# A written-out order of all steps in place of a list planner (one core, fp32 attention and gated convolution)

## Chip, core and metric

One NeuronCore of a Trainium2 chip runs the whole program. The metric is device microseconds of one execution; the median of three runs is compared. Engines: PE (TensorE, matrix products), DVE (VectorE), ACT (ScalarE), POOL (GpSimd), SP (SyncE, which only issues transfers here).

## The reference

```python
# x [4, 12800, 128], inducing [32, 128]
def mab(q, kv):
    s = scale * (q @ kv.transpose(0, 2, 1))
    s = s - s.max(-1, keepdims=True)
    a = np.exp(s)
    a /= a.sum(-1, keepdims=True) + 1e-09
    return a @ kv
h = mab(I, x)              # 32 inducing rows attend to all 12800 tokens of a batch
y = mab(x, h)              # every token attends to the 32 rows of h
gate = sigmoid(causal depthwise convolution of y, 5 taps, conv_w)
out = (gate * (y @ w_val)) @ w_out
```

So each batch is read in full (first attention) before its second attention can begin, and everything behind that works on chunks of tokens.

## The kernel before

The 12800 tokens of a batch are four strips of 3200, which lie side by side on the partitions (32 each) or are four 32-wide tiles of the PE array. A strip is cut into chunks (`SIZES`: 8 in batch 0, 7 in the others, at most 480 tokens), 29 in all. The work on a chunk consists of steps, each a Python closure that issues a few instructions on one engine:

- `load_xt`, `load_xk`: the chunk of x with channels on partitions, and with tokens on partitions. In batch 0 the second form of six chunks is made from the first (`make_xk`: PE transposes in `tp`, copies out of PSUM in `ev`).
- `s1`: scores against the inducing rows on PE; DVE copies them out and takes maxima. `gmax`: the maximum of a group of chunks. `e1`: exponential (ACT) and transpose (DVE). `h`: product with x on PE, summed per group in `H` (DVE, `acc`).
- `prep`: joins a batch's groups (ACT scales each `H`, POOL adds them, PE sums over strips) to `hT`. `prep2`, `prep3`: folds `hT` with the convolution taps and w_val into gate and value weights `W`, in two fp16 halves (`e` 0 and 1). `prep_out`: scaled w_out in two halves (`wo`) and the output scale.
- `s2`: second attention of a chunk. PE scores, then eleven steps over DVE, POOL and ACT (`tin, mx, sub, ex, sm, sa, rz, nm, tout, hi, lo`), which end in `P1` and `P2`, the high and low fp16 halves of the weights P.
- `rblock` (r0 to r29): gate products of chunk k (15 per strip, `gate_mm`) with the value products of chunk k - 1 set in (`val_mm`); then tanh of the gate banks (ACT, `th`), gate times value (DVE, `gv`), and the split into halves (`halves`: ACT `hi`, POOL `lo`).
- `outp`: output product of one strip of a chunk (three fp16 products, or one fp32 product in the last chunk), evacuation on DVE or ACT (`ev`), and store.

PSUM has four single banks, `a0` to `a3`, which nearly all of these share, and two double ones, `g0` and `g1`, for the gates (and, early, for the transposes). PE works in three tile shapes: full array, 32-column strips (`s1`, `s2`, `h`, some of `outp`) and 32-row tiles (`rblock`).

`ORDER` lists the PE work by hand, one item for each call above. `('z', k, n)` in it is `idle`: n products of a zero tile into bank g1, whose result nobody reads. `warm_up` issues eight of them before the first data. Each call appends its steps to `Plan.ops` (1547 of them); step numbers follow from that. `Plan.order` keeps the PE order of the list and lays the steps of the other engines and the banks with a table of costs: of the steps that are ready, an engine takes the one with the earliest due time, shifted by `URGE`. A load may be issued from `AHEAD` = 12 blocks ahead. Engines are fixed by the call: `OUTV` lists the evacuations that DVE does, stores go to SP's queue, loads to SP's at first and to ACT's from the first `rblock` on. `manual_schedule` then issues the steps in that order, and each engine runs its own in it.

Of the kernel before, what the change touches and what calls it, by code (L numbers as in the profile page):

```python
# [18 lines left out]
P = 128  # L19
# [18 lines left out]
PASSES = 2  # L38
LAT = dict(PE=0.3, DVE=0.06, ACT=0.045, POOL=0.09, SP=0.05, NOP=0.0)
OVER = dict(DVE=0.075, ACT=0.105, POOL=0.035)  # L40
OWN = 0.035
LAND, LAND_OUT, DEPTH = 4.0, 1.8, 2.4
BESIDE = (3.6, 1.2)
ISSUE = dict(SP=0.45, ACT=0.34)
WINDOW, LEAST = 3.4, 1.95
PAGE, ASK, NEED, LINE, FETCH = 256, 0.68, 1.8, 4.0, 2.5
SWITCH = dict(full=0.09, rows=0.115, strips=0.117)
# [7 lines left out]
class Plan:  # L55


    def __init__(self):
        self.ops = []
        self.tiles = {}  # L60
        self.users = {}
        self.item = -1
        self.urges = {}

    def urge(self, fn):
        code = fn.__code__
        if code not in self.urges:
            self.urges[code] = URGE.get(".".join(fn.__qualname__.split(".")[-3::2]), 0.0)
        return self.urges[code]

    def op(self, eng, dur, fn, deps=(), early=0.0, new=(), use=(), lag=None, kind=None, behind=(), dma=None, words=0):
        i = len(self.ops)
        self.ops.append(dict(eng=eng, dur=dur, fn=fn, deps=[d for d in deps if d is not None], early=early,
                             lag=LAT[eng] if lag is None else lag, kind=kind, behind=list(behind),
                             urge=self.urge(fn), item=self.item, dma=dma, words=words))
# [8 lines left out]
    def order(self, pe):  # L84
        ops = self.ops
        n = len(ops)
        deps = [list(o["deps"]) for o in ops]
        turn = self.turn = set()
        for tag, made in self.tiles.items():
            if tag == "a":  # L90
                continue
            bufs = BUFS[tag]
            for k, (i, key) in enumerate(made):
                if k and made[k - 1][0] != i:
                    deps[i].append(made[k - 1][0])
                    turn.add((made[k - 1][0], i))
                if k >= bufs:
                    deps[i] += [u for u in [made[k - bufs][0]] + self.users[made[k - bufs][1]] if u != i]
        for i, o in enumerate(ops):
            for j in o["behind"]:  # L100
                deps[i].append(j)
                turn.add((j, i))
        runs = []
        for i in pe:
            if not runs or ops[i]["kind"] != runs[-1][0]:
                runs.append((ops[i]["kind"], []))
            runs[-1][1].append(i)
        for k, (kind, run) in enumerate(runs):
            if kind == "either":
                near = [q[0] for q in runs[max(k - 1, 0):k + 2]]  # L110
                for i in run:
                    ops[i]["kind"] = "strips" if "strips" in near else "full"
                    ops[i]["words"] = 24 if "strips" in near else 6
        for a, b in zip(pe, pe[1:]):
            deps[b].append(a)
            ops[a]["turn"] = SWITCH[ops[a]["kind"]] * (ops[a]["kind"] != ops[b]["kind"])
        succ = [[] for _ in range(n)]
        left = [0] * n
        for i, ds in enumerate(deps):
            left[i] = len(ds)  # L120
            for d in ds:
                succ[d].append(i)
        topo, ready = [], [i for i in range(n) if not left[i]]
        cnt = list(left)
        while ready:
            i = ready.pop()
            topo.append(i)
            for s in succ[i]:
                cnt[s] -= 1
                if not cnt[s]:  # L130
                    ready.append(s)
        if len(topo) < n:
            i, seen = next(i for i in range(n) if cnt[i]), []
            while i not in seen:
                seen.append(i)
                i = next(d for d in deps[i] if d not in topo)
            raise AssertionError("a cycle in the plan: " + " <- ".join(
                f"{ops[j]['eng']} {ops[j]['fn'].__qualname__.split('.')[-3]} {[k for l in self.tiles.values() for a, k in l if a == j]}"
                for j in seen[seen.index(i):]))
        nominal, t = {}, 0.0  # L140
        for i in pe:
            nominal[i] = t
            t += ops[i]["dur"] + ops[i].get("turn", 0.0)
        best = None
        for _ in range(PASSES):
            seq, at, end, bank = self.lay(deps, succ, topo, nominal)
            if best is None or max(end) < best[0]:
                best = max(end), seq, at, end, bank
            nominal = {b: end[a] for a, b in zip(pe, pe[1:])} | {pe[0]: 0.0}
        _, seq, self.at, self.end, self.bank = best  # L150
        self.alldeps = deps
        return seq

    def lay(self, deps, succ, topo, nominal):

        ops = self.ops
        n = len(ops)
        late = [max(nominal.values()) + 30.0] * n
        for i in reversed(topo):
            late[i] = nominal.get(i, late[i])  # L160
            for s in succ[i]:
                late[i] = min(late[i], late[s] - ops[i]["dur"] - ops[i]["lag"])
        wants = [[] for _ in range(n)]
        held = {}
        holds = [[] for _ in range(n)]
        for i, key in self.tiles.get("a", []):
            wants[i].append(key)
            held[key] = 1 + len(self.users[key])
            for u in [i] + self.users[key]:
                holds[u].append(key)  # L170
        open_ = [(0.0, b) for b in range(BUFS["a"])]
        bank, gone = {}, {}
        free, bus = dict.fromkeys(("PE", "DVE", "ACT", "POOL"), 0.75), 1.45
        line, slow, ran = 0.0, 8.0, []
        told, asked, held_up = 0, [], 0
        end = [0.0] * n
        at = [0.0] * n
        avail = {}
        left = [len(ds) for ds in deps]
        pools = {}  # L180
        for i in range(n):
            if not left[i]:
                pools.setdefault(ops[i]["eng"], []).append((ops[i]["early"], i))
        seq = []
        while len(seq) < n:
            best = None
            for e, lst in pools.items():
                if not lst:
                    continue
                if e == "ACT":  # L190
                    lst[:] = [(max(r, bus - DEPTH) if ops[i]["dma"] and ops[i]["dma"][1] == "load" else r, i) for r, i in lst]
                start = max(free.get(e, 0.0), min(r for r, _ in lst))
                if e == "PE":
                    w = len(wants[lst[0][1]])
                    if w > len(open_):
                        continue
                    if w:
                        start = max(start, open_[w - 1][0])
                if best is None or start < best[0]:
                    best = (start, e)  # L200
            start, e = best
            lst = pools[e]
            _, i, r = min((late[i] - ops[i]["urge"], i, r) for r, i in lst if r <= start + 1e-9)
            lst.remove((r, i))
            at[i] = start
            end[i] = start + ops[i]["dur"] + ops[i].get("turn", 0.0)
            if e == "PE":
                if start > slow and sum(b - max(a, start - WINDOW) for a, b in ran if b > start - WINDOW) < LEAST:
                    slow = start + WINDOW
                work = end[i] - start  # L210
                if 8.0 < start < slow:
                    end[i] = start + (2 * work if 2 * work < slow - start else work + (slow - start) / 2)
                begun, w, work = told, ops[i]["words"], end[i] - start
                told += w
                while told > PAGE * (len(asked) + ASK):
# [46 lines left out]
def tile_kernel(ctx: ExitStack, tc: tile.TileContext, xt, xk, indT_in, w64, out):  # L262
# [121 lines left out]
    def sp(dur, fn, new, use=(), free=False):  # L384

        i = op("ACT" if blocks else "SP", dur, fn, [ago()], 0.0, new, use, behind=[] if free else queue[-1:], dma=(dur, "load"))
        if not blocks and not free:
            queue.append(i)
# [833 lines left out]
```

## Time and profile before

| | us |
|---|---|
| median of 3 runs | 277.09 |
| lowest, highest | 276.94, 277.39 |
| profiled execution, span from the first to the last instruction | 275.9 |
| PE, DVE, POOL, ACT busy in it | 265.0, 230.7, 207.6, 197.1 |
| HBM read, written | 48.56 MB, 26.21 MB |

The profile is of one execution. Its span is 1.2 us below the median of the runs. Busy times count the instructions of an engine, not the time in which it issues transfers; the end of a matmul is modelled.

### The profile page before, as it was taken

To read this page: it belongs to the slowest core of one execution; us is meant where nothing else is said; L and a number is where in the kernel's file an instruction comes from. 1 tells how busy PE (TensorE), PEld (TensorE's weight loads), DVE (VectorE), ACT (ScalarE), POOL (GpSimd) and SP (SyncE) were. 2 spreads that over 40 slices of the span, in tenths; PEclk is the share of its full clock that TensorE was granted. 3 is DMA by queue.
4 is the path that set the end of the run, shared out by engine and by line. 5 is a ranking of instruction groups with operands and counts; after the bars stand their busy time and mean duration, and the time that the engine had idled before them with its cause. 6 is when DMAs were issued, how large, how long until landed. Compare 5 with 4: busy or idle time off the path is not lost.

```text
span 275.9 us, 11249 instructions
## 1 busy us (share of the span) xinstructions
PE 265.0 (96%) x4730; PEld 148.4 (54%) x4730; DVE 230.7 (84%) x542; ACT 197.1 (71%) x298; POOL 207.6 (75%) x236
## 2 busy tenths in 40 slices
PE   7999998999999999999999999999999999999993
PEld 2568445557646655475445564665554456544541
DVE  1569799879999989898899998979999998896761
ACT  2366369669849786787677877957778887777763
POOL 2000477986699999966986999877999999999550
PEclk9999999999999999999999999999999999999998
DMA  7999999998999799969999879425443234344447
GB/s 250 424 415 383 416 423 380 385 318 293 323 372 403 227 349 393 397 213 369 343 352 323 297 224 377 150 76 209 150 154 122 85 138 155 133 163 152 149 180 281
DMA packets 35378, 75.49 MB, mean 274 GB/s; under 512 B 2816, under 2 KB 26752, under 8 KB 35328
## 3 DMA queue, kind: packets, MB, share of 16 engines
q1 hardware_dynamic: 19120, 42.03, 39.9%
q10 hardware_dynamic: 16208, 32.75, 34.5%
q8 instruction: 37, 0.61, 0.9%
q14 instruction: 13, 0.11, 0.1%
HBM read 48.56 MB, written 26.21 MB: 271 GB/s over the span
## 4 chain that ended last, share of the span: by engine, by line
PE 87%; DVE 4%; ACT 4%; DMA 2%; issue 1%; POOL 1%; SPq 0%; ACTq 0%; DVEq 0%
PE g L845 29%; PE a L958 23%; PE a L751 8%; PE a L553 7%; PE a L487 7%; PE a L854 6%; DMA xt<-in_xt_dram 2%; PE g L462 2%; ACT xk L467 1%; PE g L1010 1%; PE a L677 1%; ACT ss L533 1%; PE a L948 1%; DVE os L971 1%; DVE tg L914 1%
## 5 line engine op out<-in xcount | busy, mean ns | idle before, releaser
L932 POOL TENSOR_TENSOR gl<-tg,gh 128x960 f16<-128x960 f32 (+4 forms) x56 | 104.7, 1882 | 13.1 <-PE a L958 7.5
L845 PE MATMUL g<-P,W 32*128 32x480 f16 (+4 forms) x1740 | 103.1, 345 | 0.8 <-issue 0.7
L845 PEld LDWEIGHTS <-W 32*128 32x128 f16 x1740 | 53.8, 92 | 38.9 <-issue 10.0
L914 DVE SCALAR_TENSOR_TENSOR tg<-tg,a 128x480 f32<-128x480 f32 (+4 forms) x116 | 64.6, 598 | 6.5 <-PE a L854 5.3
L927 ACT CAST gh<-tg 128x960 f16<-128x960 f32 (+4 forms) x56 | 51.9, 928 | 25.5 <-DVE tg L914 23.8
L958 PE MATMUL a<-gh,wo 128*32 128x448 f16 (+6 forms) x632 | 63.1, 348 | 1.0 <-DVE tg L914 1.0
L904 ACT ACTIVATE tg<-g,gsc 128x960 f32<-128x960 f32 (+4 forms) x58 | 55.4, 991 | 3.4 <-PE g L845 3.1
L958 PEld LDWEIGHTS <-wo 128*32 128x32 f16 (+1 forms) x948 | 35.5, 97 | 37.4 <-issue 16.4
L971 DVE TENSOR_SCALAR os<-a,osc 128x480 f32<-128x480 f32 (+4 forms) x64 | 41.1, 667 | 4.9 <-PE a L958 4.7
L958 PE MATMUL a<-gl,wo 128*32 128x448 f16 (+6 forms) x316 | 43.1, 348 | 0.0
L854 PE MATMUL a<-P,W 32*128 32x480 f16 (+4 forms) x348 | 42.1, 344 | 0.6 <-issue 0.5
L831 POOL TENSOR_TENSOR P<-pt,P 128x480 f16<-128x480 f32 (+4 forms) x29 | 29.9, 1036 | 2.3 <-ACT P L824 1.4
L813 POOL TENSOR_TENSOR e<-e,z 128x480 f32<-128x480 f32 (+4 forms) x29 | 27.2, 938 | 5.8 <-DVE z L806 3.6
L973 ACT ACTIVATE os<-a,osc 128x480 f32<-128x480 f32 (+4 forms) x44 | 26.8, 627 | 6.4 <-PE a L958 5.9
L768 POOL TENSOR_TENSOR e<-e,m 128x480 f32<-128x480 f32 (+4 forms) x29 | 27.2, 940 | 5.0 <-DVE m L762 3.3
L553 PE MATMUL a<-xk,et 128*32 128x129 f32 x800 | 29.2, 274 | 0.7 <-DVE tg L914 0.7
L553 PEld LDWEIGHTS a<-xk,et 128*32 128x32 f32 x800 | 25.0, 109 | 6.8 <-issue 1.9
L751 PE MATMUL a<-xt,hT 128*32 128x480 f32 (+4 forms) x232 | 28.0, 541 | 0.0
L487 PE MATMUL a<-xt,indT 128*32 128x480 f32 (+4 forms) x232 | 26.8, 538 | 1.1 <-DMA xt<-in_xt_dram 0.7
L495 DVE TENSOR_SCALAR_CACHE_REDUCE ss<-a 128x480 f32<-128x480 f32 (+4 forms) x29 | 17.2, 600 | 9.2 <-PE a L487 9.1
L774 ACT ACTIVATE e<-e 128x480 f32<-128x480 f32 (+4 forms) x29 | 16.6, 572 | 8.4 <-POOL e L768 8.2
L824 ACT CAST P<-pt 128x480 f16<-128x480 f32 (+4 forms) x29 | 16.2, 561 | 7.2 <-DVE pt L819 5.5
(107 smaller groups left out, 282.5 us busy)
## 6 DMA issues: line engine op xcount, KB each, us to landing
out_dram<-os SPq DMA_DIRECT2D x52, 240.0 KB, 3.1
xt<-in_xt_dram ACTq DMA_DIRECT2D x11, 960.0 KB, 7.4
out_dram<-os SPq DMA_DIRECT2D x44, 224.0 KB, 4.0
xk<-in_xk_dram ACTq DMA_DIRECT2D x9, 967.5 KB, 9.2
xk<-in_xk_dram ACTq DMA_DIRECT2D x7, 903.0 KB, 8.8
xt<-in_xt_dram SPq DMA_DIRECT2D x6, 960.0 KB, 9.9
xt<-in_xt_dram ACTq DMA_DIRECT2D x5, 896.0 KB, 7.5
xk<-in_xk_dram SPq DMA_DIRECT2D x4, 903.0 KB, 13.3
```

The source lines that it names most:

```text
L487: T.matmul(s[32 * r:32 * r + 32, :n], c_["indT"], x[:, o:o + n // 32, r, :], start=True, stop=True)
L553: T.matmul(t[32 * s:32 * s + 32, :P + 1], st["et", b, c][:, 32 * i:32 * i + 32], st["xk", b, q][:, m + i, :], start=j < R, stop=j >= len(b ...
L751: T.matmul(s[32 * r:32 * r + 32, :n], st["hT", b], x[:, m:m + nb, r, :], start=True, stop=True)
L831: G.tensor_tensor(st[p2][:, o:o + n], st[qk][:, :n], st[p1][:, o:o + n], ALU.subtract)
L845: T.matmul(st[f"g{r // 2}", b, c][:, r % 2, :n], st["W", b][q, w, k, :], st[("P1", "P2")[e]][q, o:o + n], start=u == 0, stop=u == len(taps ...
L854: T.matmul(st["a", "v", b, c, r][:, :n], st["W", b][q, w, TAPS, :], st[("P1", "P2")[e]][q, o:o + n], start=u == 0, stop=u == 2)
L904: S.activation(t[:, :, :n], st[f"g{p}", b, c][:, :, :n], AF.Tanh, scale=st["gsc", b])
L914: V.scalar_tensor_tensor(t, t, 1.0, st["a", "v", b, c, r][:, :n], ALU.add, ALU.mult)
L927: S.copy(sb(pw, g1, [P, 2, CW], F16)[:, :, :n], st[tg][:, :, :n])
L932: G.tensor_tensor(sb(pw, g2, [P, 2, CW], F16)[:, :, :n], st[tg][:, :, :n], st[g1][:, :, :n], ALU.subtract)
L958: T.matmul(t[o:o + wide], w[:, e, o:o + wide], st[g][:, q, :n], start=(e, g) == (0, g1), stop=g == g2)
L971: V.tensor_scalar(o, a, st["osc", b], None, ALU.mult)
```

## The change

The planner, its costs and `URGE` are removed. In their place stand three literals: `SEQ`, the numbers of all 1547 steps in the order in which they are issued; `BANKS`, the `a` bank of each step that opens one; `ELSE`, the engine of 120 steps whose engine differs from that of the call. The PE order is now that of `SEQ` too, and differs from `ORDER` (renamed `WORK`, which now only numbers the steps).

`ELSE` does the following:

- all nine `idle` steps of `ORDER` become nothing (16 products of zeros); `warm_up` stays
- output evacuations: 23 from DVE to ACT, 17 from ACT to DVE
- stores: 34 from SP's queue to ACT's, 2 from ACT's to SP's; of the 34, 17 store what DVE has evacuated
- `sa` of 12 chunks from POOL to DVE
- copies of `make_xk`: three from ACT to DVE, one from DVE to ACT; `acc`: three from DVE to ACT; `prep3.f7`: two from ACT to DVE; `prep2.g1`: one from POOL to DVE

In `prep` of batch 0 the last of the four groups is no longer scaled and added by ACT and POOL. PE sums the first three (`f3`) and adds the fourth with a scaled `pick` into the same bank (`f6`). The halves of the last chunk but one go to buffers of tag `ss` instead of `gh` and `gl`. Loads have no limit of blocks any more. In the new `SEQ` the weights' transfer is issued fifth on SP's queue (ninth before), and the second chunk of batch 0 is loaded ahead of the third, the fourth ahead of the fifth.

```diff
-        for i, o in enumerate(ops):
-            for j in o["behind"]:
...
-        for _ in range(PASSES):
-            seq, at, end, bank = self.lay(deps, succ, topo, nominal)
...
+        banks = iter(BANKS)
+        self.bank = {key: int(next(banks)) for i in SEQ for key in ops[i]["new"] if key[0] == "a"}
+        return SEQ
...
+    def issue():
+        return S if plan.now == "ACT" else nc.sync
...
+        last = len(gs) - 1 if b in JOIN else len(gs)
...
-        for g in gs[1:]:
+        for g in gs[1:last]:
...
+        def add(H, w, first, end):
+            t = pt(key) if first else st[key]
+            T.matmul(t[:, :M], H[:, :P], w, start=first, stop=end, skip_group_check=True)
+            T.matmul(t[:, M:2 * M], H[:, P:].broadcast_to([P, P]), w, start=first and end, stop=end, skip_group_check=True)
+
         def f3():
...
+            add(st[Hs[last - 1]], c_["pick"], True, last == len(gs))
...
+        if b in JOIN:
+            pf = ("pf", b)
+
+            def f5():
+                G.tensor_scalar(sb(pw, pf, [P, M]), c_["pick"], st[f_][:, last:last + 1], None, ALU.mult)
+
+            j = op("POOL", 0.26, f5, [i0, i_const], [pf], [f_])
+
+            def f6():
+                add(st[Hs[last]], st[pf], False, True)
...
+    def split(b, c, p):
+
+        late = seqs.index((b, c)) >= len(seqs) - 1 - SPARE
+        return ("tg", b, c, p), ("ss" if late else "gh", "hi", b, c, p), ("ss" if late else "gl", "lo", b, c, p)
...
+            if plan.now == "PE":
+                t = pt(key, (P, 2, 512))[:, 0]
+                for _ in range(n):
+                    T.matmul(t, c_["zero"][:, :P], c_["zero"], start=True, stop=True)
...
+SPARE = 1
+JOIN = (0,)
...
+SEQ = [
+    5, 17, 1, 20, 0, 2, 13, 4, 38, 75, 29, 62, 9, 3, 69, 72, 32, 88, 111, 10, 125, 6, 11, 174, 190, 7, 12, 33, 201,
...
+ELSE = {
+    8: "NOP", 11: "DVE", 16: "NOP", 24: "ACT", 34: "DVE", 36: "DVE", 50: "ACT", 124: "NOP", 140: "NOP", 141: "NOP",
```

## Rows read from the trace of the kernel before

**Rows 1.** Page of the profile: span, busy time, chain by engine.

```profile
span 275.9 us, 11249 instructions
...
PE 265.0 (96%) x4730; PEld 148.4 (54%) x4730; DVE 230.7 (84%) x542; ACT 197.1 (71%) x298; POOL 207.6 (75%) x236
...
PE 87%; DVE 4%; ACT 4%; DMA 2%; issue 1%; POOL 1%; SPq 0%; ACTq 0%; DVEq 0%
```

**Rows 2.** Busy time by stretches (us; instructions; granted clock; DMA share; GB/s).

```profile
35.00:40.00 5.00, 4.89 (x128) 2.21 (x122) 4.65 (x16) 3.00 (x6) 3.63 (x8) 1.00 1.01 422
40.00:45.00 5.00, 4.46 (x112) 2.58 (x103) 4.74 (x14) 4.07 (x9) 4.08 (x7) 1.00 1.02 390
45.00:50.00 5.00, 3.59 (x90) 2.65 (x84) 4.82 (x15) 3.86 (x9) 3.56 (x6) 1.00 1.05 383
50.00:60.00 10.00, 10.00 (x216) 5.69 (x212) 8.19 (x20) 6.84 (x12) 8.35 (x11) 1.00 1.02 349
...
80.00:120.00 40.00, 39.66 (x767) 22.89 (x758) 37.07 (x85) 33.22 (x51) 38.02 (x41) 1.00 0.93 338
...
270.00:276.00 6.00, 1.40 (x6) 0.48 (x4) 0.36 (x1) 1.75 (x3) 0.00 (x0) 0.84 0.72 266
```

**Rows 3.** Groups of instructions by form: products of zeros inside the run.

```profile
L1010 PE MATMUL g<-zero 128*128 128x512 f16 x16 | 5.0, 382 | 0.2
```

**Rows 4.** Timeline (start, length in us), end of batch 0's sum.

```profile
28.66 1.53 POOL L596 TENSOR_TENSOR H<-H 128x129 f32<-128x129 f32 x3 [5.74 <-ACT H L587]
...
28.80 0.28 DVE L563 COPY H<-a 128x129 f32<-128x129 f32 x1
...
29.11 0.41 ACT L591 ACTIVATE H<-H,f 128x129 f32<-128x129 f32 x1 [0.23 <-DVE H L563]
...
30.25 0.41 PE L602 MATMUL a<-pick,H 128*128 128x32 f32 x2
...
30.50 0.39 PE L603 MATMUL a<-pick,H 128*128 128x32 f32 x2
...
31.53 0.19 DVE L611 TENSOR_TENSOR hT<-a,rz 128x32 f32<-128x32 f32 x1
```

**Rows 5.** Timeline, second weight copy and start of r0.

```profile
35.96 1.47 PE L1010 MATMUL g<-zero 128*128 128x512 f16 x4
...
37.93 0.80 ACT L687 COPY W<-a 128x768 f16<-128x768 f16 x1 [0.37 <-PE a L677]
38.01 0.49 POOL L831 TENSOR_TENSOR P<-pt,P 128x160 f16<-128x160 f32 x1
38.02 0.39 ACTq L420 DMA_DIRECT2D xt<-in_xt_dram  x1
...
38.56 0.60 PE L1010 MATMUL g<-zero 128*128 128x512 f16 x2
...
39.10 1.14 PE L845 MATMUL g<-P,W 32*128 32x128 f16 x60
```

**Rows 6.** Timeline, third P chunk, last tanh before r2, start of r2.

```profile
42.11 0.64 DVE L819 STREAM_TRANSPOSE pt<-e 128x480 f32<-128x480 f32 x1
...
47.92 0.79 ACT L904 ACTIVATE tg<-g,gsc 128x640 f32<-128x640 f32 x1
...
49.76 0.39 PE L845 MATMUL g<-P,W 32*128 32x480 f16 x4 [0.68 <-issue]
```

**Rows 7.** Groups by form on DVE and ACT: count, busy us, mean ns.

```profile
L757 DVE STREAM_TRANSPOSE e<-a 128x480 f32<-128x480 f32 x17 | 11.4, 673 | 0.6 <-PE a L516 0.2
...
L762 DVE TENSOR_REDUCE m<-e 128x15 f32<-128x480 f32 x17 | 10.9, 643 | 0.2
...
L824 ACT CAST P<-pt 128x480 f16<-128x480 f32 x17 | 10.0, 589 | 5.5 <-DVE pt L819 3.8 <-PE a L854 1.6
...
L495 DVE TENSOR_SCALAR_CACHE_REDUCE ss<-a 128x448 f32<-128x448 f32 x11 | 6.6, 609 | 1.9 <-PE a L487 1.9
```

**Rows 8.** Timeline of the tail: the wait before the last output products.

```profile
262.80 0.56 PE L958 MATMUL a<-gh,wo 128*128 128x480 f16 x2 [0.97 <-DVE tg L914]
```

More of the change, by code (lines that the diff above doesn't have):

```diff
@@ L37 @@
 SCALE = 1.0 / math.sqrt(P)
[L38 to L47, printed above, removed]
 COST = dict(
@@ L61, in __init__, with op @@
         self.users = {}
[L62 to L71, printed above, removed]
+        self.now = None
+    def op(self, eng, dur, fn, deps=(), new=(), use=(), lag=None, kind=None, dma=None, words=0, alt=None):
         i = len(self.ops)
-        self.ops.append(dict(eng=eng, dur=dur, fn=fn, deps=[d for d in deps if d is not None], early=early,
-                             lag=LAT[eng] if lag is None else lag, kind=kind, behind=list(behind),
-                             urge=self.urge(fn), item=self.item, dma=dma, words=words))
+        self.ops.append(dict(eng=ELSE.get(i, eng), first=eng, dur=dur, fn=fn, deps=[d for d in deps if d is not None], new=list(new),
+                             use=list(use), lag=lag, kind=kind, dma=dma, words=words, alt=alt or {}))
         for key in new:
@@ L82, in op, with order @@
         return i
-    def order(self, pe):
+    def order(self):
         ops = self.ops
[L86 to L98, printed above, removed]
-        for i, o in enumerate(ops):
-            for j in o["behind"]:
-                deps[i].append(j)
-                turn.add((j, i))
-        runs = []
[L104 to L107, printed above, removed]
+        assert sorted(SEQ) == list(range(len(ops)))
+        runs = []
+        for i in SEQ:
+            if ops[i]["eng"] == "PE":
+                if not runs or ops[i]["kind"] != runs[-1][0]:
+                    runs.append((ops[i]["kind"], []))
+                runs[-1][1].append(i)
         for k, (kind, run) in enumerate(runs):
@@ L123, in order @@
[L123 to L139, printed above, removed]
@@ L369, in tile_kernel, with two, copy @@
     ix = {}
+    def two():
+        return V if plan.now == "DVE" else G
+    def copy(dst, src):
+        if plan.now == "ACT":
+            S.copy(dst, src)
+        else:
+            V.tensor_copy(dst, src)
     def sb(pool, key, shape, dt=F32, pad=None):
@@ L380, in tile_kernel, with load @@
     blocks = []
-    queue = []
[L384 to L388, printed above, removed]
-        return i
-    def ago():
-        return blocks[-AHEAD] if len(blocks) >= AHEAD else None
+    def load(dur, fn, new, use=()):
+        return op("ACT" if blocks else "SP", dur, fn, [], new, use, dma=(dur, "load"))
+    def issue():
+        return S if plan.now == "ACT" else nc.sync
     def wid(b, c):
@@ L412, in load_xt @@
         own = key[2] == c
-        early = S if blocks else nc.sync
         def f():
@@ L426, in load_xk, with made, xk_tile, get @@
+    def made(b, c):
+        return max(SIZES[b][c] // 32 - LOADED.get((b, c), NB), 0)
+    def xk_tile(b, c):
+        q, m = shares(b, c)
+        key = ("xk", b, q)
+        new = key not in plan.users
+        def get():
+            if key not in st:
+                sb(pxk, key, [P, CW // 32, P + 1])
+            return st[key]
+        return key, m, get, [key] * new, [key] * (not new)
     def load_xk(b, c):
         n = SIZES[b][c] // 32
+        lo = made(b, c)
+        s = 1 if lo else PARTS[(b, c) >= (1, 4)][1]
@@ L440, in make_xk @@
+        ix["xk", b, c, 1] = load((1.04 if (b, c) >= (1, 4) else 1.0) * (n - lo) * 66048 / BW, f, new, use)
     def make_xk(b, c, eng):
-        n = SIZES[b][c] // 32
+        n = made(b, c)
         xkey, o = xt_of(b, c)
-        q, m = shares(b, c)
-        key = ("xk", b, q)
+        key, m, get, new, use = xk_tile(b, c)
         last = []
         def ones():
-            if q == c:
-                sb(pxk, key, [P, CW // 32, P + 1])
-            G.memset(st[key][:, m:m + n, P:], 1.0)
-        i0 = op("POOL", 0.13, ones, [], 0.0, [key] * (q == c), [key] * (q != c))
+            G.memset(get()[:, m:m + n, P:], 1.0)
@@ L454, in make_xk @@
+        i0 = op("POOL", 0.13, ones, [], new, use)
         for g in range(0, n, 8):
@@ L753, in s2 @@
         i = PE(COST["s"] * n + 0.015, f, [ix["xt", b, c, u], ix["hT", b]], [key], [xkey, ("hT", b)], "strips")
+        soon = dict(DVE=cost("dve", n) + 0.05) if b == 0 and c < 3 else None
         def tin():
```

449 lines of the change are left out of this document (136 added, 313 removed), and 71 rows, old and new, of the table SEQ.

## The prediction, made before the changed kernel had run

> **What bounds the kernel now.** First read the busy shares and the chain [rows 1]: TensorE (PE) is busy 265.0 of 275.9 us and 87% of the chain is PE, 1% "issue" (time that no wait explains). Then the stretches [rows 2]: from 50 us on PE shows 10.00 of 10 and 40.00 of 40 (39.66 in 80 to 120), so there only less PE work, or denser PE work, can shorten the run. Before that it is different: in 35 to 50 us PE shows 4.89, 4.46 and 3.59 of 5 while VectorE (DVE) shows 4.65, 4.74 and 4.82. The ramp, in which batch 0 is turned from raw loads into the first gate blocks, waits for DVE chains, and part of what PE shows there is products of zeros [rows 3]. Third, the timeline of the ramp at three places: the end of the sum over batch 0 [rows 4], the start of the first gate block r0 [rows 5], and the start of r2, after which PE hardly stops [rows 6]. Last the tail: one wait of 0.97 us at 262.80 [rows 8], then steady matmuls to the end.
>
> The profiled execution has a span of 275.9 us [rows 1]; the runs' median, 277.09, lies 1.2 us above it. Sums are made on the span and carried to the median by that 1.2.
>
> The literal list names steps by the number that the work list gives them, so each engine's new queue can be read off and set beside the old one. It changes six things.
>
> **1. Sum of the last group joined on PE.** Before: the last accumulate of batch 0 starts at 28.80, ScalarE (ACT) scales it at 29.11 for 0.41, POOL adds it last in a train of three (28.66 to 30.19), and PE starts at 30.25 [rows 4]. Now the scale and add of that group are gone; POOL makes a 128x32 scaled `pick` earlier, and PE does two products of three groups and two of the fourth. Those two more cost about 0.25 (the two shown start 0.25 apart: 30.25 and 30.50). The three-group sum must still pass ACT and POOL: without its last third the POOL train of 1.53 ends about 29.65, so the first two products start about 0.6 earlier, less 0.25: gain 0.35. The bound above is the whole 30.25 - 28.80 - 0.28 - 0.25 = 0.9; the bound below is nothing, because DVE's new queue puts four accumulates and the weight maxima directly ahead of the last accumulate. I take 0.5: the list also sets ACT's scales of the first groups between two tile copies that both stood ahead of them.
>
> **2. Sixteen zero products gone.** They are busy 5.0 us [rows 3]. What they cost is what waited behind them. Four of them stand from 35.96 to 37.36 between the two weight transposes, the second of which ACT copies at 37.93 to 38.73; two stand at 38.56, and r0 starts at 39.10, although the low half of its P was ready at 38.50 (POOL 38.01 + 0.49) [rows 5]. Without them r0 could start at 38.5: 0.6. Elsewhere they lie in time that PE waits anyway. This 0.6 is r0's alone and is no term of its own: r2, below, is held by other things.
>
> **3. New queues in the ramp.** r2 needs the third P chunk, and both gate banks, which ACT's tanh of r1 sets free. In the old trace the chunk's transpose ran on DVE at 42.11 to 42.75, but ACT did the second tanh only at 47.92 to 48.71, behind four exponentials, a cast and loads, and r2 ran from 49.76 [rows 6]. In the new queue DVE does more ahead of that transpose: one maximum step of batch 1 (0.61), one transpose from PSUM (0.67), one maximum (0.64), one transpose of batch 1 (priced like the other, 0.67) [rows 7], and two short ones, some 0.4: 3.0 us. DVE was full there [rows 2], so the transpose ends 3.0 later against hT, the result of step 1: 42.75 - 0.5 + 3.0 = 45.25. But ACT then has the cast (0.59) and directly behind it both tanh (0.79 each): 45.25 + 0.6 + 1.6 = 47.4. In the old trace 1.05 lies between the second tanh and r2, of which 0.68 is issue time; with the other 0.37 r2 starts at about 47.8, a gain of 2.0. Bounds: nothing, if the lower half of P (POOL, behind more work now) is late by 2; and 3.5, if r2 and what follows also close the 1.95 us that PE was idle in 40 to 50.
>
> Late next: behind r2, POOL's new queue has two subtractions, three short steps and one low half ahead of the low half of the output weights, which the first output product needs. If that comes late PE waits there; up to 0.5 us of loss stays inside the range. I keep 2.0, steps 1 and 2 included.
>
> **4. The steady part.** Counting the changes of tile shape on PE (32-row gates, 32-column strips, full array) from the end of r1 on, both orders have 64, so nothing is won there by construction. The Trainium skill says in TensorEngine Tiling (Array Packing), Key Properties, that a change of tiling mode drains TensorE; by that rule too the two orders would stand equal. Engines: 12 short POOL steps go to DVE, 23 output evacuations from DVE to ACT and 17 the other way, so DVE, which shows 37.07 of 40 in 80 to 120, gives six evacuations away and takes twelve short steps: eased by little. What can change is the spacing. The chain's "issue" share is 1% (2.8 us), and such small waits are there to be won or made; bounds +2.0 and -1.5 (loss). I take a gain of 0.5, a fifth of that share.
>
> **5. Stores.** 34 output stores go from SP's queue to ACT's and two come back. The issue of a load there takes ACT 0.39 us [rows 5]; a store's is taken as the same, net 32 x 0.39 = 12.5 us of ACT time, and 17 of the 34 wait for an evacuation on DVE, with casts, tanh and evacuations queued behind them on ACT. In 80 to 120 ACT is busy 33.22 of 40, issues not counted. About seven of the stores fall there, 2.7 us, into some 3 us that are left once the loads' issues (about nine) are counted. So I cost it at nothing, with up to 2.7 us of loss if that cover is gone.
>
> The Trainium skill, in DMA: Bandwidth & Descriptors, Issuing engines are not separate DMA queues, says that DMAs of all engines run on the same 16 DMA engines and that issuing from several saves only the issue time. By it these stores buy no bandwidth; no run here shows it yet.
>
> **6. Tail.** The last chunk but one gets buffers of its own for its halves. The wait at 262.80 is for DVE to free a bank [rows 8] and its chain (tanh, then DVE) stays. One more output product stands ahead of r28 instead of behind r29, which moves work and removes none. The last evacuation has 352 columns, not 480. Gain 0.2, bounds -0.5 and +0.8.
>
> **Sum.** 2.0 + 0.5 + 0.2 = 2.7: span 273.2, median **274.4 us**. Its own range is 273.0 to 276.5.
>
> **Rivals.**
> - *More is won* (271.5): the ramp gives 3.5, the steady part 2.0, the tail 0.3. For it: PE's waits in 40 to 50 and its 1% of issue time. Against: equal mode changes, and a DVE that is full in the ramp.
> - *Given back* (276.9): PE comes two microseconds earlier to a stretch where POOL shows 38.02 and DVE 37.07 of 40; if they set the pace there, PE waits and only the tail is left. Against: in the next stretches PE never waits for them in the old trace, and POOL gets less to do.
> - *ACT is blocked* (278.3): a store on ACT that waits for DVE holds back tanh and with it a gate bank. Decides if the waits of the 17 stores come to more than 2.7 us where PE has nothing else ready; with 3.9, some 0.23 each, the time is 274.4 + 3.9.
> - *The clock falls* (281): the granted clock was 1.00 throughout with the zero products in, and 0.84 in the last 6 us, in which PE was busy 1.40 [rows 2]. If it went to the lower of its two levels in 35 to 50 us without them, the PE work there (4.89 less 2.07 of zeros, plus 4.46 and 3.59: 10.9 us) takes 21.8 in 15: 6.8 late, less the 2.7 of the sum, so 4.1 over the old time. Decides from 2.7 us of uncovered work at the lower level. Against: the stretches of the ramp keep 72% and more of PE busy. TensorE: Matmul & The Clock Gate in the Trainium skill (Part 1) says that the clock gate falls back to half rate when the array has been idle, which speaks against taking fillers out; the old trace agrees only in its last stretch.
>
> **Chances.** Forecast 0.50, more won 0.26, given back 0.11, ACT blocked 0.08, clock 0.05. A measurement of this kernel can tell 0.2% (0.55 us) from no change. Faster takes the first two and a little of the third: 0.78; same (276.5 to 277.6) 0.10; slower 0.12. The range reaches from 271.3, under the second case, to 277.5, over the third.
>
> **What would show it.** Step 1: hT is written by 31.3 (31.53 to 31.72 before). Step 2: no product of `zero` behind 5 us and PEclk 1.00 in every early stretch. Step 3: r2's gate matmuls begin at 47 to 48.5, both tanh of 640 columns just ahead. Step 4: from there to the tail the same distance as before within 1.5. Step 5: ACT idle on DVE no longer than before. The prediction is wrong if r2 starts at 49 or later, or if the distance from r2 to the end grows.

## The result, and the profile after

The changed kernel takes 279.15 us (median of 13 runs, 277.01 to 281.63) beside 276.95 for the kernel before (276.52 to 277.76): ratio 1.0065, 95% interval [1.0044, 1.0086]. It is slower by 2.2 us; the prediction said 274.4. Its runs also spread over 4.6 us where those of the kernel before spread over 1.2. (The intervals leave out runs more than 1.5% above a kernel's fastest, which cuts off the longest times of a kernel that spreads this far; so medians and ranges stand beside them.)

The page of the changed kernel: span, busy time, the chain by engine, and the queue of PE's instructions (packets, MB).

```profile
span 277.8 us, 11199 instructions
...
PE 263.1 (95%) x4736; PEld 145.8 (52%) x4736; DVE 233.9 (84%) x551; ACT 198.8 (72%) x302; POOL 205.0 (74%) x222
...
q8 instruction: 37, 0.61, 0.9%
...
PE 77%; DMA 9%; DVE 6%; ACT 4%; issue 2%; ACTq 1%; POOL 1%; SPq 0%; DVEq 0%
```

Against [rows 1] PE is busy 1.9 us less in a span 1.9 us longer; "issue" has doubled to 2%. The stretches, columns as in [rows 2]:

```profile
35.00:40.00 5.00, 3.04 (x60) 1.50 (x64) 3.03 (x10) 2.37 (x6) 3.44 (x6) 1.00 1.01 415
40.00:45.00 5.00, 4.14 (x124) 2.46 (x116) 4.52 (x15) 2.81 (x6) 2.77 (x5) 1.00 0.77 256
45.00:50.00 5.00, 3.42 (x97) 2.60 (x85) 4.75 (x12) 4.74 (x12) 3.72 (x6) 1.00 1.04 388
50.00:60.00 10.00, 9.81 (x187) 5.62 (x190) 8.29 (x22) 5.88 (x11) 6.43 (x10) 1.00 0.69 213
80.00:120.00 40.00, 39.10 (x750) 20.84 (x746) 37.18 (x88) 31.17 (x50) 33.35 (x35) 1.00 0.98 348
```

In 35 to 40 us PE, DVE and ACT fall back together, to 3.04, 3.03 and 2.37 of 5 (4.89, of which 2.07 were zeros, 4.65 and 3.00 before). Now the timeline at the places of [rows 4 to 6]; the PE rows are put together by line, and what stands in brackets is the idle time ahead of a row and what the profile holds to have ended it.

```profile
30.49 0.19 DVE L474 TENSOR_TENSOR hT<-a,rz 128x32 f32<-128x32 f32 x1
...
33.69 0.85 PE L540 MATMUL a<-ident,w 128*32 128x128 f16 x48
36.96 0.96 PE L323 MATMUL a<-xt,indT 128*32 128x448 f32 x8 [2.42 <-DVE z L656]
...
45.03 0.63 DVE L681 STREAM_TRANSPOSE pt<-e 128x480 f32<-128x480 f32 x1
46.20 1.48 ACT L766 ACTIVATE tg<-g,gsc 128x640 f32<-128x640 f32 x2
47.78 0.38 PE L707 MATMUL g<-P,W 32*128 32x480 f16 x4
...
48.13 0.29 PE L716 MATMUL a<-P,W 32*128 32x320 f16 x1
50.19 0.29 PE L716 MATMUL a<-P,W 32*128 32x320 f16 x1 [1.76 <-issue]
```

hT comes 1.04 earlier (30.68 against 31.72 in [rows 4]). The transpose of the third P chunk (it ends at 45.66; 45.25 was forecast) and both tanh (at 47.68; 47.4) stand about where the prediction put them, and r2 begins at 47.78. But behind its ninth product it stops for 2 us, and it is done at about 53.4, as before (53.3). Ahead of r0 there is a second hole, of 2.42. The two rows at 48.13 and 50.19 belong to one accumulation: nothing in the program stands between them to be waited for.

What ends that hole is seen in the view of the DMA queues. PE's instructions come through q8, 16 KB a packet; 37 packets for the 4736 products and 4736 weight loads of the page are some 256 instructions each. I call one packet a code page. Narrowing the window finds the packet of this hole, and none between 42 and 47.7:

```profile
q10 hardware_dynamic: 233, 0.41, 100.9%
q8 instruction: 1, 0.02, 6.2%
```

This is 47.70 to 48.78; loads fill the engines beside it (100.9%). PE goes on at 50.19, 2.48 after the packet's start. The hole that ends at 36.93 (with the weight load of the product at 36.96) has its packet at 34.43, 2.50 earlier. The kernel before had the same, smaller: packets at 40.90 and 47.28, and after them holes that end at 43.42 (inside r1, 0.47 idle) and at 49.76, which is the 0.68 of "issue" in [rows 6]: 2.52 and 2.48 later.

Counting instructions shows what these places have in common. Busy time and counts up to each hole's end (products, then weight loads):

```profile
0.00:26.90 26.90, 24.58 (x346) 16.04 (x347) 15.92 (x51) 13.96 (x22) 3.69 (x26) 1.00 0.95 383
26.90:36.92 10.02, 6.77 (x126) 3.88 (x125) 7.55 (x31) 3.65 (x9) 4.99 (x12) 1.00 1.01 413
36.92:50.18 13.26, 10.60 (x253) 6.56 (x254) 10.49 (x29) 8.34 (x18) 8.20 (x15) 1.00 0.94 347
```

346 + 347 = 693 instructions up to the first hole (0.35 of "issue" at 26.91), 251 more up to the second, 507 more, two pages, up to the one in r2. So a border comes every 252 to 254 products and weight loads.

### The profile page after: what moved, and what is told of

Same layout as the page of the kernel before. It is cut to its first block, busy times and chain, and to the rows that moved or that the text cites. A ratio compares the mean times of both kernels' runs of the same rounds, so it can differ in the third digit from the quotient of the medians.

```text
span 277.8 us, 11199 instructions
## 1 busy us (share of the span) xinstructions
PE 263.1 (95%) x4736; PEld 145.8 (52%) x4736; DVE 233.9 (84%) x551; ACT 198.8 (72%) x302; POOL 205.0 (74%) x222
## 4 chain that ended last, share of the span: by engine, by line
PE 77%; DMA 9%; DVE 6%; ACT 4%; issue 2%; ACTq 1%; POOL 1%; SPq 0%; DVEq 0%
PE g L707 26%; PE a L825 21%; PE a L397 8%; PE a L323 6%; DMA xk<-in_xk_dram 5%; PE a L716 5%; PE a L611 5%; DMA xt<-in_xt_dram 3%; PE g L301 3%; PE a L861 1%; ACT gh L794 1%; DVE os L838 1%; ACT os L840 1%; ACT tg L766 1%; DVE tg L776 1%
## 5 line engine op out<-in xcount | busy, mean ns | idle before, releaser
L799 POOL TENSOR_TENSOR gl<-tg,gh 128x960 f16<-128x960 f32 (+4 forms) x54 | 101.2, 1878 | 9.6 <-PE a L825 3.2
L707 PEld LDWEIGHTS <-W 32*128 32x128 f16 x1740 | 51.8, 92 | 42.5 <-issue 11.1
L776 DVE SCALAR_TENSOR_TENSOR tg<-tg,a 128x480 f32<-128x480 f32 (+4 forms) x116 | 66.4, 600 | 8.7 <-PE a L716 6.6
L794 ACT CAST gh<-tg 128x960 f16<-128x960 f32 (+4 forms) x54 | 50.0, 928 | 21.9 <-DVE tg L776 19.2
L825 PE MATMUL a<-gh,wo 128*32 128x448 f16 (+6 forms) x636 | 61.2, 349 | 1.5 <-DVE tg L776 0.7
L825 PEld LDWEIGHTS <-wo 128*32 128x32 f16 (+1 forms) x966 | 36.3, 97 | 37.7 <-issue 17.6
L825 PE MATMUL a<-gl,wo 128*32 128x448 f16 (+6 forms) x318 | 42.0, 348 | 0.0
L840 ACT ACTIVATE os<-a,osc 128x480 f32<-128x480 f32 (+4 forms) x54 | 33.4, 630 | 6.7 <-PE a L825 5.8
L838 DVE TENSOR_SCALAR os<-a,osc 128x480 f32<-128x480 f32 (+4 forms) x54 | 34.7, 665 | 3.9 <-PE a L825 3.3
L369 ACT ACTIVATE ss<-ss,ng 128x480 f32<-128x480 f32 (+4 forms) x29 | 17.9, 657 | 2.5 <-DVE ng L359 2.4
L716 PEld LDWEIGHTS <-W 32*128 32x128 f16 x348 | 15.9, 92 | 7.2 <-issue 0.9
```

Of the source, the lines that this page charges most:

```text
L707: T.matmul(st[f"g{r // 2}", b, c][:, r % 2, :n], st["W", b][q, w, k, :], st[("P1", "P2")[e]][q, o:o + n], start=u == 0, stop=u == len(taps ...
L716: T.matmul(st["a", "v", b, c, r][:, :n], st["W", b][q, w, TAPS, :], st[("P1", "P2")[e]][q, o:o + n], start=u == 0, stop=u == 2)
L776: V.scalar_tensor_tensor(t, t, 1.0, st["a", "v", b, c, r][:, :n], ALU.add, ALU.mult)
L794: S.copy(sb(pw, g1, [P, 2, CW], F16)[:, :, :n], st[tg][:, :, :n])
L799: G.tensor_tensor(sb(pw, g2, [P, 2, CW], F16)[:, :, :n], st[tg][:, :, :n], st[g1][:, :, :n], ALU.subtract)
L825: T.matmul(t[o:o + wide], w[:, e, o:o + wide], st[g][:, q, :n], start=(e, g) == (0, g1), stop=g == g2)
```

## The experiments

Times beside the kernel before, run on the same chips (its medians 276.95 to 276.96):

| kernel | median us (range) | ratio, 95% interval |
|---|---|---|
| changed | 279.15 (277.01 to 281.63) | 1.0065 [1.0044, 1.0086] |
| changed again (9) | 278.25 (275.99 to 282.80) | 1.0025 [0.9999, 1.0051] |
| 1 three loads late | 281.27 (277.67 to 281.75) | 1.0125 [1.0083, 1.0167] |
| 2 one load late | 278.30 (276.15 to 283.83) | 1.0021 [0.9993, 1.0050] |
| 3 z on POOL | 279.20 (275.69 to 281.32) | 1.0025 [0.9999, 1.0051] |
| 4 stores on SP | 277.95 (275.12 to 282.71) | 1.0004 [0.9979, 1.0028] |
| 5 border moved by 24 | 276.33 (275.67 to 278.39) | 0.9979 [0.9959, 0.9999] |
| 6 loads paced | 277.62 (275.62 to 280.29) | 1.0012 [0.9985, 1.0038] |
| 7 evacuations back | 279.81 (278.94 to 285.47) | 1.0101 [1.0064, 1.0139] |
| 8 before, no zeros | 277.42 (275.81 to 278.56) | 1.0011 [0.9987, 1.0034] |
| 10 border by 24, stores on SP | 275.23 (274.49 to 275.83) | 0.9931 [0.9908, 0.9953] |
| 11 border by 48 | 275.20 (274.63 to 276.29) | 0.9932 [0.9910, 0.9954] |
| 12 as 10, z on POOL | 275.44 (274.77 to 276.35) | 0.9942 [0.9921, 0.9963] |
| 13 three wide products | 278.87 (275.13 to 281.08) | 1.0036 [1.0004, 1.0068] |
| 14 border by 48, stores on SP | 274.65 (274.04 to 276.00) | 0.9923 [0.9897, 0.9948] |
| 15 before, border by 20 | 276.60 (276.42 to 277.31) | 0.9993 [0.9980, 1.0005] |

**1 and 2. Loads held back.** Is it the queue of loads that a page's packet waits in?

```diff
 SEQ, experiment 1 (2 moves 422 alone)
-165, 304, 208   184, 293, 243   245, 422, 250
+165, 208        184, 243        245, 250
-249, 232
+249, 304, 293, 422, 232
```

> The changed kernel with three x loads (batch 1 chunks 6 and 4, batch 2 chunk 0) issued behind both tanh of r1, some 4 to 5 us later. Theory 'code page': the 2.06 us hole inside r2 (48.13 to 50.19) is PE waiting for its next 16 KB of instructions, whose packet started only at 47.71, behind four loads issued from 41.54 to 43.68. Without three of them the packet starts within 2.5 us of 43.65, the hole shrinks to 0.3 us or less, r2 ends some 2 us earlier, and the time falls from 279.15 by 1.5 to 2.1: to about 277.3. Rival 'data': the hole waits for a tile that the trace does not show; it stays at 1.8 to 2.1 and the time stays at 279.2, or rises if the late loads are missed at 54 us.

> The changed kernel with only the last of the four loads (batch 2 chunk 0) issued behind both tanh of r1. 'Code page': one load fewer stands ahead of the packet only if it would have been served before it; a load of 0.98 MB takes 2.3 us at 420 GB/s, so the packet starts between 45.4 and 47.7 and the hole is 0 to 2.0, between that of the other run and that of the changed kernel; time 277.3 to 279.2. 'Data': hole and time as in the changed kernel, 279.2.

Experiment 1: r2's hole shrank to 0.69 ("code page" expected 0.3 or less; it ends at count 1443, eight short of the border, so it may be another wait), but the time rose by 2 instead of falling: a miss. Its two longest holes of "issue" stand at later borders; whether the moved loads made them is not shown, since the unchanged list has holes at the same two counts in experiment 9:

```profile
68.26 0.31 PE L825 MATMUL a<-gh,wo 128*32 128x320 f16 x2 [0.96 <-issue]
...
74.69 0.58 PE L323 MATMUL a<-xt,indT 128*32 128x448 f32 x4 [1.67 <-issue]
```

The instruction at 74.69 is number 2465, four pages behind 1451. In experiment 2 the hole behind the weight transposes was absent, though nothing ahead of it was changed: its page came at 29.4 instead of 34.4. So one trace of a kernel that spreads this far is one draw; "data" is not refuted by these two alone (experiment 5 does that).

**3 and 4. z back on POOL; stores back on SP.** `ELSE` holds 107 entries, not 120.

```diff
 ELSE, experiment 3: twelve entries out
-237: "DVE", 268: "DVE", 432: "DVE", ...
 ELSE, experiment 4: 36 entries out
-317: "ACT", 342: "ACT", ... 1535: "SP", 1546: "SP",
```

> The changed kernel with the 12 short steps on z (z plus 1e-9, times a constant) back on POOL, at the same places of the order. Theory 'z waits for POOL': on DVE they took 0.11 to 1.53 us each, the long ones ending with the POOL instruction that ran beside them, and the one at 87.10 (1.53) starts the loss of 1.8 us against the kernel before in 80 to 110 us. On POOL each takes 0.21 to 0.22; the loss goes and the time falls from 279.15 by 1 to 2, to about 277.5. Rival 'stores': the loss comes from the stores on ACT; the time stays at 279.2. Second rival: POOL is late by its extra work where it stands at 8 to 9 tenths, and the time rises by up to 1.

> The changed kernel with the 34 stores back on SP and the two back on ACT, at the same places of the order. 'Stores': ACT's issues (0.36 us each, about 12 us of ACT) and its waits for evacuations on DVE make tanh and evacuations late from 80 us on; without them 1 to 2 us come back, to about 277.5. 'z waits for POOL' and 'code page': nothing changes, 279.2 within 0.6, since ACT idles 79 us and the hole in r2 lies ahead of the first store.

Neither settles anything within such a spread: 279.20 and 277.95. In both r2's hole is there again (1.84 of idle, ended at 49.74, in experiment 4). Experiment 12 later takes the z edit without the spread, 275.44 beside 275.23: the z theory falls.

**5. The border moved.** Twelve products of 8 columns, whose result nobody reads, go where PE waits for POOL anyway.

```diff
 idle.f
-                for _ in range(n):
-                    T.matmul(t, c_["zero"][:, :P], c_["zero"], start=True, stop=True)
+                for _ in range(12):
+                    T.matmul(t[:, :8], c_["zero"][:, :P], c_["zero"][:, :8], start=True, stop=True)
 ELSE
-    124: "NOP",
 SEQ
-123, 202, 136, 138
+123, 202, 124, 136, 138
```

> The changed kernel with 12 products of zeros, 8 columns wide, just ahead of the joined sum of batch 0, where PE waits 1.04 us (27.71 to 28.76) for POOL: 24 instructions more on PE, 0.6 us of work inside a wait. 'Code page': the holes stay at the same count of PE instructions, so each falls 24 instructions earlier in the program: the one inside r2 moves out of r2 into the products of h just ahead of it, and r2's first product starts at 50 or later instead of 47.8, with no hole inside; the one in the weight transposes moves ahead of the second transpose. Time 279.2 within 1. Rival 'data': the 24 instructions end inside the wait, r2 starts at 47.8 and stops behind its ninth product as before.

The place came out as "code page" said. Counts up to the hole's end, then the timeline:

```profile
0.00:46.39 46.39, 42.27 (x725) 26.26 (x726) 32.51 (x108) 24.19 (x44) 15.45 (x48) 1.00 0.98 393
```

```profile
46.40 0.41 PE L397 MATMUL a<-xk,et 128*32 128x129 f32 x3 [1.26 <-issue]
46.74 0.38 PE L707 MATMUL g<-P,W 32*128 32x480 f16 x4
...
48.37 2.00 PE L707 MATMUL g<-P,W 32*128 32x480 f16 x36
50.30 0.30 PE L825 MATMUL a<-gh,wo 128*32 128x128 f16 x8
```

725 + 726 = 1451 again, but the hole now stands among the products of h, and r2 runs through in 3.6 us. The count decides where PE stops, and not what the product reads: "data" falls. The time did not come out as I expected (279.2): with 24 idle instructions the median is 2 to 3 us lower, and nine of ten runs lie within 1.2 us. The tenth, 278.39, is the profiled one; beside the hole above it has one more, nine borders further on:

```profile
104.62 0.36 PE L707 MATMUL g<-P,W 32*128 32x448 f16 x2 [1.61 <-issue]
```

**6. Loads paced.** Eight of SP's loads to ACT and four of ACT's later, the same bytes.

```diff
 SEQ, behind the steps named: 125 (93), 190 (120), 174 (109), 201 (169), 126 (200), 175 (158),
      300 (182), 304 (164), 293 (188), 191 (249), 202 (256), 422 (235)
 ELSE
+    125: "ACT", 190: "ACT", 174: "ACT", 201: "ACT", 126: "ACT", 175: "ACT", 191: "ACT", 202: "ACT",
```

> The changed kernel with twelve loads of batches 1 and 2 spread over the ramp: the eight that SP issues between 10 and 28 us go to ACT's queue, each some 5 to 10 us ahead of its use, and four of ACT's go some 4 us later. Bytes are the same; what is issued and not yet landed falls from 4.9 MB at 30 us to about 2. 'Code page, by depth': a page's packet waits behind the bytes outstanding, so the pages of 34.4, 40.9 and 47.7 come 2 us or more earlier, the holes at 34.3, 42.4 and 48.1 (2.6, 1.2 and 2.1 us) shrink by half or more, and the time falls by 2 to 4, to 275 to 277. 'Code page, by a fixed wait': with anything outstanding a page takes some 4 us, whatever the depth; holes shrink by 1 at most and the time falls by 0 to 1.5. 'Data': no hole changes; time 279 or more, since ACT issues eight loads more (0.4 us each).

277.62, with holes still there:

```profile
46.88 0.29 PE L716 MATMUL a<-P,W 32*128 32x320 f16 x1 [0.65 <-issue]
...
65.92 0.31 PE L825 MATMUL a<-gh,wo 128*32 128x320 f16 x2 [0.82 <-issue]
...
72.63 0.96 PE L323 MATMUL a<-xt,indT 128*32 128x448 f32 x8 [1.94 <-issue]
```

The pages came earlier than in the first trace (28.2, 36.0 and 44.4 us for 34.4, 40.9 and 47.7), but so they do when the unchanged list is run again (29.6, 37.9 and 44.5; experiment 9), and the holes of that trace (0.54, 0.55, 1.39) are no longer than the three here. So a shorter queue of loads closed none of them, which speaks against "by depth". The 0.6 to 1.5 below the changed kernel's two medians lie inside its spread; "by a fixed wait" fits but is not shown.

**7 and 8. Evacuations back; the kernel before without zero products.**

```diff
 ELSE, experiment 7: 40 entries out
-347: "ACT", 410: "ACT", ... 309: "DVE", 420: "DVE", ...
 the kernel before, idle.f, experiment 8
-            t = pt(key, (P, 2, 512))[:, 0]
-            for _ in range(n):
-                T.matmul(t, c_["zero"][:, :P], c_["zero"], start=True, stop=True)
+            pass
```

> The changed kernel with the 40 output evacuations that had changed their engine back where they were (23 on DVE, 17 on ACT), at the same places of the order. Theory 'order': the loss of about 1.5 us against the kernel before in 80 to 110 us is the literal order's own, in which DVE is at 9.7 of 10 in 80 to 100 us; then nothing is won: 279 to 280.5, since DVE gets six evacuations (4 us) more. Rival 'engines': the swaps made evacuations late and PE waits for their banks; then the loss in 80 to 110 shrinks by 1 or more and the time falls to 278.

> The kernel before with its 16 zero products behind the warm-up left out and nothing else changed: one part of the change alone. 'Code page': r1 and r2 are held by the arrival of PE's pages (holes of 0.77 at 42.65 and 0.75 at 49.01 in the kernel before), whose borders move 32 instructions later in the program; r0 may start 0.5 earlier, r2 ends within 0.7 of 53.3, and the time stays at 277.0 within 0.7. Rival 'zeros hold PE': the products stand in the way of r0 and what follows; the time falls by 0.6 to 2, to 275 to 276.4. Rival 'clock': the granted clock falls below 1.0 in the ramp and the time rises by 2 or more.

Experiment 7: 279.81, so the swaps are not what costs. Its one trace points the other way: it has a single hole at a border (1.27) and still a span of 277.6, with 2.9 us in which PE waits for DVE and ACT behind 75 us where experiment 14 has 1.1. Experiment 8: 277.42 beside 276.95, no difference, with a range of 2.7 us instead of 1.2 to 2.2. Left out alone, the zero products win nothing at the median, and the clock stays up (0.997 over the profiled run).

**9 to 12. The changed kernel again, and the border once more.**

```diff
 9: no edit.   10: experiments 4 and 5 together.   12: 3, 4 and 5 together.
 11: experiment 5 with
-                for _ in range(12):
+                for _ in range(24):
```

> The changed kernel once more, beside the runs with the border moved, on their chip. If 24 idle instructions on PE really won 2.8 us, it gives 278.5 to 279.5 here too, and the border-moved kernel stays near 276.3. If what differs is when a page's packet is served in a call (the third page came at 34.4 in four of the first five traces of this list, at 28 to 30 in the five others), it gives 277 to 278 here and the third page comes early.

> The 12 narrow products of zeros ahead of the joined sum, and the 34 stores back on SP and two on ACT. The stores alone gave 277.95 beside 279.15, the narrow products alone 276.33. If both are their own, the time is near 275.2, below the kernel before by 1.5; if the stores' 1.2 was the spread of the page arrivals, it is 276.3 as with the products alone.

> The changed kernel with 24 narrow products of zeros instead of 12 at the same place, 48 instructions more. 'Code page': the border falls another 24 instructions earlier, among the products of h ahead of r2; r2 itself stays without a hole, its first product comes as soon as the page does, at 46.5 to 50, and the time is within 0.6 of that with 12 products. If the idle instructions won by something else (PE kept busy ahead of the sum), 24 win as much or more.

> The 12 narrow products of zeros, the stores back on SP, and the 12 short steps on z back on POOL. If the waits of z for POOL cost DVE time that PE waits for in 80 to 110 us, this is 0.5 to 1.5 below the run without the z edit; if not, the same within 0.6.

The changed kernel gave 278.25 and its spread of 6.8 us; with 24 or 48 instructions more, 275.2 to 275.4 and 1.3 to 1.7. Of these, experiment 11 has nothing else changed: 275.20 beside 278.25 on one chip. The second trace of the changed kernel shows what was put down to DVE at 36.96:

```profile
33.79 0.85 PE L540 MATMUL a<-ident,w 128*32 128x128 f16 x48
34.46 0.94 PE L323 MATMUL a<-xt,indT 128*32 128x448 f32 x8
...
46.81 0.29 PE L716 MATMUL a<-P,W 32*128 32x320 f16 x1 [0.54 <-issue]
...
71.74 0.96 PE L323 MATMUL a<-xt,indT 128*32 128x448 f32 x8 [1.39 <-issue]
```

Here the page came at 29.6 and the product ran at 34.46, two microseconds before the z step (36.48 here) that the first trace names. The lead of 2.5 us was lost again at 46.81 and, in instruction 2465, at 71.74. With 48 more, r2 starts at 45.72 with no idle time ahead, and no hole of "issue" stands in 40 to 80 (experiment 11):

```profile
45.72 0.90 PE L707 MATMUL g<-P,W 32*128 32x480 f16 x4
```

**13 to 15. The number of instructions, or the time they fill?**

```diff
 13: experiment 5 with
-                for _ in range(12):
-                    T.matmul(t[:, :8], c_["zero"][:, :P], c_["zero"][:, :8], start=True, stop=True)
+                for _ in range(3):
+                    T.matmul(t, c_["zero"][:, :P], c_["zero"], start=True, stop=True)
 14: experiments 4 and 11 together
 15: the kernel before, idle.f
-            for _ in range(n):
+            for _ in range(12 if k == 14 else n):
+                m = 8 if k == 14 else 512
```

> The changed kernel with 3 products of zeros of 512 columns where the narrow runs have 12 or 24 of 8 columns: some 0.64 us of PE, but 6 instructions. 'Code page': a border moves by 6 instructions only and stays inside r2; the time is that of the changed kernel, 278.2 to 279.2, with its spread. 'PE kept busy': work ahead of the sum is what wins; then 275.2 to 276.4 as with the narrow ones.

> The changed kernel with 24 narrow products of zeros and the stores back on SP. With 24 products and the stores on ACT it gave 275.20, with 12 and the stores on SP 275.23. If stores on ACT cost 1 us, it gives about 274.2; if they cost nothing, 275.2 within 0.5, still below both kernels.

> The kernel before with the two wide products of zeros ahead of its sum of batch 0 replaced by 12 narrow ones: 20 instructions more on PE and nothing else. 'Code page': its holes at the borders (0.77 in r1, 0.75 at the start of r2) move 20 instructions earlier in the program; they were small, so the time moves little, 276.3 to 277.7. If narrow products win by themselves, it falls by 2 or more as in the changed kernel, to 275 or below.

Three wide products fill the same wait with 6 instructions: 278.87, with a range of 6 us, as the changed kernel, and the hole at count 1451 (0.51) is inside r2 again. So it is the number. The kernel before, whose holes were small, gains 0.4 from 20 more, inside its noise. Experiment 14 is the fastest of all, 274.65, 2.3 below the kernel before:

```profile
span 272.9 us, 11268 instructions
...
45.25 0.64 PE L397 MATMUL a<-xk,et 128*32 128x129 f32 x15 [0.40 <-issue]
45.83 0.38 PE L707 MATMUL g<-P,W 32*128 32x480 f16 x4
```

Its 0.55 below experiment 11 could be the stores' issues on ACT (12.5 us by the prediction's estimate), but the intervals overlap; it stays open.

All traces side by side. The third column adds up PE's idle time of 0.2 us and more ahead of a product at a border (counts 693, 945, 1197, 1451 and on by 254, two more or less; in the kernel before and experiments 8 and 15 they lie 6 higher):

| trace | span, us | idle at borders, us | span less it |
|---|---|---|---|
| changed | 277.8 | 4.5 | 273.3 |
| changed again (9) | 276.4 | 2.5 | 273.9 |
| 1 | 279.6 | 5.3 | 274.3 |
| 2 | 276.3 | 3.6 | 272.7 |
| 3 | 277.9 | 4.4 | 273.5 |
| 4 | 277.9 | 5.9 | 272.0 |
| 6 | 276.8 | 3.4 | 273.4 |
| 13 | 276.1 | 1.9 | 274.2 |
| 7 | 277.6 | 1.3 | 276.3 |
| 5, border by 24 | 276.6 | 2.9 | 273.7 |
| 10, border by 24 | 273.1 | 1.3 | 271.8 |
| 12, border by 24 | 273.7 | 0.9 | 272.8 |
| 11, border by 48 | 273.2 | 0.0 | 273.2 |
| 14, border by 48 | 272.9 | 0.4 | 272.5 |
| before | 275.9 | 1.1 | 274.8 |
| 8, before | 274.1 | 0.0 | 274.1 |
| 15, before | 274.7 | 0.0 | 274.7 |

Leaving experiment 7 aside, the changed kernel and its variants have spans from 272.9 to 279.6, and 271.8 to 274.3 without that idle time: the holes carry most of the loss and of the spread. The median of these, 273.3, beside 274.1 to 274.8 in the last three rows puts the order itself at 0.8 to 1.5 us won (an estimate: where a hole goes, another wait may take part of its place). Of the nine traces with the border in place (13 among them, which moves it by 6), all but 7 lose time at count 945 or at one of 1959 to 2465; none of the five with it moved by 24 or 48 does. Why 24 instructions are enough for that is not shown.

## Why the prediction was wrong

Steps 1 and 2 held in the trace: hT at 30.68 (31.3 was the bound), no product of zeros behind 5 us, a granted clock of 1.00 in every early stretch. Step 1 won 1.04 where I took 0.5. Step 2 gave r0 nothing: it began at 39.63, 0.5 later than in [rows 5], behind the hole of 2.42; in experiment 14, where that hole is absent, it begins at 36.94 and goes on at 37.86 (38.5 was forecast).

The step that failed is in part 3: "In the old trace 1.05 lies between the second tanh and r2, of which 0.68 is issue time; with the other 0.37 r2 starts at about 47.8, a gain of 2.0." r2 did start at 47.78. But I left the 0.68 out as if it would go, without a reason, and it was the end of a wait for a code page: the sum had no term for these waits. The new order brings PE to the border of that page earlier than the page comes, and the 2.0 were paid back inside r2 (2.06 from product to product), besides 2.42 ahead of r0. Idle time at borders up to r2 is 0.35 + 2.42 + 1.76 = 4.5 us, against 0.47 + 0.68 = 1.15 before. That r2 began at 47.78 is partly luck: it did so with 2.42 of idle time ahead of r0, and in experiments 11 and 14 it begins at 45.72 and 45.83. The code had warned: `PAGE, ASK, NEED, LINE, FETCH` in `Plan.lay` of the kernel before price just this wait, by counts of PE instructions, and the change takes that pricing out with the planner. I compared the queues that it made and not the prices it made them by.

Part 4 forecast a gain of 0.5 behind r2; from r2's start to the end the run took 229.98 instead of 226.17, 3.8 more, which is one of the two signs that the prediction had named for being wrong. Of these 2.06 are r2's hole. The other 1.7 lie behind it: PE is busy 39.10 of 40 in 80 to 120 us where [rows 2] show 39.66, with small waits (0.18 and 0.25 for ACT's evacuations, 0.30 for a load). Part of it is the order's own: in experiments 14 and 11, with no hole at a border behind r2's start, that distance is 227.0 and 227.5, so 0.9 and 1.3 longer than before where parts 4 and 6 had it 0.7 shorter. z on DVE and the swapped evacuations are not the cause (12, 7). In part 6 the wait of 0.97 in the tail shrank to 0.69, about as forecast.

Part 5 held as far as it can be told: ACT waits no longer for DVE ahead of its casts (19.2 us, 23.8 before), and about 1 us at most hangs on the stores (medians 0.55 and 1.1 lower with them on SP, 14 beside 11 and 10 beside 5, on unlike chips). Of the rivals, "ACT is blocked" (278.3) came nearest in its number, but experiment 11, with those stores on ACT, is at 275.20. "Given back" (276.9) had the outline, an early PE that loses what it won, but the wrong place: neither POOL nor DVE set the pace, and PE's own instructions did. The clock did not fall, though the prediction's "72% and more" of busy PE counted the zeros in 35 to 40 us; without them it was 2.82 of 5.

With the border moved by 48 and the stores back, the same order and the same join give a span of 272.9 and 274.65 us; the sum had 273.2 and 274.4. That the total agrees is luck in part, for two errors cancel: the ramp gave 3.9 (r2 at 45.83 instead of 49.76) where I took 2.0 with a bound of 3.5, and from r2 on 0.9 was lost where I had 0.7 won. One term was missing: the pages, some 3 us of the median (experiment 11 beside 9).

Open: why the third page came at 34.1 to 34.6 us in four of the first five traces of the changed list and at 28.2 to 30.8 in the others, with the same instructions and loads ahead of it in most of them. Open as well: what delays a packet. The DMA engines were full of loads at most of the holes, but no run took the loads away.

## What to carry to other kernels

"Issue" on PE ahead of a product with nothing to wait for can be a wait with a cause, and so can a wait put down to a step that was long done: look for the instruction queue's packet some 2.5 us before it, and count PE's instructions to the next border. An order of many small products can be bound by the arrival of its own code, here while loads filled the DMA engines; then a few idle instructions inside a wait can be worth more than the work they stand beside, and one profiled run is not enough to see it. When a change freezes what a planner made, carry over the planner's prices, not only its list.

## What the runs showed of the hardware

The Trainium skill says in Runtime: NRT & Kernel Launch, Instruction fetch mechanics, that instructions come in blocks of 16 KiB, 256 of them, and that crossing a block costs one queue step, "mostly hidden". The block's size agrees with the 37 packets; hidden it is not in the first 75 us here (and once at 104.62, in experiment 5): 2.42 us of idle at one border. At every hole of the table the packet had started 2.2 to 2.7 us before PE's next product.

A short step on DVE can last until the POOL instruction beside it ends. The first row is POOL's, the second DVE's:

```profile
86.59 2.01 POOL L799 TENSOR_TENSOR gl<-tg,gh 128x960 f16<-128x960 f32 x1
```

```profile
87.10 1.53 DVE L662 TENSOR_SCALAR z<-z 128x15 f32<-128x15 f32 x1
```

Both end at 88.6. The seven steps of this shape took 4.7 us on DVE, two of them 0.16 and 0.17 each; on POOL one takes 0.22. This agrees with the Trainium skill, SBUF — State Buffer, Who interferes with whom (DVE's two-port modes and GpSimd exclude each other for a whole instruction). Here it cost no time that can be measured (12).
